# Sliding-window attention and a gated MLP on one core: two tiles of 384 tokens, one of 256 and seven of 512 instead of four of 384 and six of 512

## The chip, the core and the metric

The kernel runs on one core of one Trainium2 chip. The metric is the device time of one execution in microseconds (us). The core has five engines that run side by side and wait for one another by semaphores: TensorE (PE, matrix products into the accumulation memory PSUM), VectorE (DVE), ScalarE (ACT), GpSimd (POOL) and SyncE (SP). Transfers run on 16 DMA engines; here POOL issues all loads after the first two, and SP issues nearly all stores.

## The reference

Attention over 8 batches and 8 heads, 576 positions and 64 dimensions per head: each position sees itself and the 63 positions before it. Then a gated MLP over the 4608 tokens.

```python
scores = scale * np.matmul(q, k.transpose(0, 1, 3, 2))
rel = pos[:, None] - pos[None, :]
mask = (rel >= 0) & (rel < 64)
attn = softmax(np.where(mask, scores, -1e9))
x = np.matmul(attn, v)                       # (8, 8, 576, 64) -> (4608, 512)
gate = np.maximum(x @ w_gate, 0.0)           # 512 -> 1536
return (gate * (x @ w_val)) @ w_out          # 1536 -> 512
```

Inputs and output are fp32; the kernel computes in fp16 with fp32 accumulation.

## The kernel before

**Tiles.** The tokens are worked through in ten tiles. The first four hold 384 tokens each (two "units" of 192, or three windows of 64), the other six 512 each (two "quads" of four windows). A batch has nine windows, so tiles and batches don't line up.

**Attention.** q and k of a batch are loaded (`qk_load`, L167) and turned by DVE so that dimensions lie on the partitions (`qk_trans`, L185: four transposes per batch, k and q for each half of the heads). Both results are double-buffered by batch (`qTs`, `kTs`). v is loaded by `v_load` (L191), and `v_spread` copies it (L200, L202) so that each window finds the keys before it as well; from unit 4 on POOL makes these copies. For a window, PE computes the transposed scores (L233), ACT takes the exponential (L267 for units, L352 for quads), DVE multiplies with a band of ones (L272, L356), and PE multiplies with v (L293, L371), where a further column of ones gives the sum. DVE takes the reciprocal (L307, L386), multiplies (L317, L391) and turns the result (L327, L396) into `xt`, the input of the MLP with its dimensions on the partitions. A wide tile's result takes two pairs of PSUM banks and a further bank for what is left over ("rest").

**MLP.** `hidden` computes for each of 12 blocks of 128 hidden columns the products with w_gate and w_val (L468, four matmuls each), ACT's relu (L453) and DVE's product of both (L456). The matmuls stream all tokens of the tile. Where they are 256 or fewer, a PSUM bank holds two blocks and ACT and DVE take both at once (`w = 512 // n`). `output` multiplies each 128 tokens with w_out (L482, 12 matmuls of 512 columns), ACT copies the result out (L489), and SP stores it.

**Order.** The order of all instructions is written out by hand. `Weaver` keeps a clock in us that follows PE's work as planned: each matmul group adds its price, and `W.at(T, fn)` puts a piece of attention work in a heap with a due time. Before each group, everything due is emitted. So due times decide where in PE's stream the scores and values of the next tile stand, and in which order DVE, ACT and POOL, which run their own streams in program order, take masks, transposes, copies and gates. `pair` plans a tile of 384 and `plan_wide` a tile of 512; `loads` and `wide_loads` plan a batch's q, k and v. `ahead(t)` plans tile t + 1 and the loads of tile t + 2 when tile t begins. `ready(t)` emits what is left of tile t's attention before PE starts its hidden layer. Tile 2 is planned with due times given as constants (`pair(2, 56.0, 59.0, 62.5)`), and batch 2's loads too (`loads(3, 70.0)`: q and k at 58, v at 64, transposes at 70.0, 71.4, 72.8 and 74.2).

Of the kernel before, what the change touches and what calls it, by code (L numbers as in the profile page):

```python
# [10 lines left out]
FP32 = mybir.dt.float32  # L11
FP16 = mybir.dt.float16
# [32 lines left out]
def kernel(  # L45
# [10 lines left out]
    nc = tc.nc  # L56
    B, H, S, D = q.shape
    DM = H * D
    DF = moe_w_gate.shape[1]
    NT = B * S  # L60
    U = 192
    UB = S // U
# [4 lines left out]
    scale = 1.0 / float(D) ** 0.5  # L67
    TT = 2 * U
    WT = 512
    NS = 4  # L70
    NL = (NT - NS * TT) // WT
    assert NT == NS * TT + NL * WT and TT % 128 == 0
    starts = [TT * t for t in range(NS)] + [NS * TT + WT * t for t in range(NL)]
    widths = [TT] * NS + [WT] * NL

    consts = ctx.enter_context(tc.tile_pool(name="consts", bufs=1))
    persist = ctx.enter_context(tc.tile_pool(name="persist", bufs=1))
# [57 lines left out]
    def xt_tile(t):  # L135
        if t not in xts:
            xts[t] = x_sb.tile([128, NC, WT], FP16, name="xt")
        return xts[t]
# [75 lines left out]
    def one_bank(name):  # L214
        return f_ps.tile([128, 512], FP32, name=name, tag="h")

    def two_banks(name):
        return a_ps.tile([128, 2, 512], FP32, name=name, tag="a")
# [32 lines left out]
    def u_st(u, hhs=(0, 1)):  # L251
        d = units.setdefault(u, {})
        if "st" not in d:
            st_tiles(u)
        run_rows([[st_block(d["st"][g][:, U * hh + 64 * w:U * hh + 64 * w + 64], g, hh, UB * u + w, "biased" in d)
                   for hh in hhs for w in range(UB)] for g in range(G)])
        return 0.29 * len(hhs)
# [44 lines left out]
    def u_recip(u, hhs=(0, 1)):  # L302
        d = units[u]
        if "r" not in d:
            d["r"] = a_n.tile([128, 2, SB, 1], FP32, name="r")
        if len(hhs) == 2:
            nc.vector.reciprocal(d["r"], d["both"][:, :, 0:SB * VW].rearrange("p a (s c) -> p a s c", c=VW)[:, :, :, D:D + 1])  # L307
        else:
            hh = hhs[0]
            nc.vector.reciprocal(d["r"][:, hh], pv_of(d, u, hh)[:, :, D:D + 1])  # L310

    def u_norm(u, hh):

        d = units[u]
        if "x" not in d:
            d["x"] = a_n.tile([128, 2, SB, 2, D // 2], FP16, name="x")
        nc.vector.tensor_tensor(d["x"][:, hh], pv_of(d, u, hh)[:, :, 0:D].rearrange("p s (c e) -> p s e c", e=2),  # L317
                                d["r"][:, hh, :, :, None].to_broadcast([128, SB, 2, D // 2]), MUL)
# [11 lines left out]
            normed[0] = (u + 1) // 2 - 1  # L330

    QW = 4
    WS = 2 * WT // 64
    BS = 512 // VW
    quads = {}
    wides = {}

    def q_window(qd, i):
        return NS * TT // 64 + QW * qd + i

    def q_st(qd):

# [14 lines left out]

    def t_pv(t):

        d = wides[t] = {"pv": [two_banks("pv") for _ in range(2)], "rest": one_bank("pv"),  # L360
                        "x": a_n.tile([128, 2, WS, 2, D // 2], FP16, name="xw"), "r": a_n.tile([128, 2, WS, 1], FP32, name="rw")}
        for qh in range(2):
            qd = 2 * (t - NS) + qh
            for hh in range(2):
                for i in range(QW):
                    b, vw = divmod(q_window(qd, i), NG)
                    for s in range(2):
                        n = 2 * (QW * qh + i) + s
                        to = d["pv"][hh][:, n // BS, VW * (n % BS):] if n < 2 * BS else d["rest"][:, VW * (2 * hh + n - 2 * BS):]
                        for j in range(G):  # L370
                            nc.tensor.matmul(to[32 * j:32 * j + 32, 0:D + 1],  # L371
                                             quads[qd]["p"][j][:, QW * hh + i, 32 * s:32 * s + 32],
                                             v16s[b % 2][:, vw, G * hh + j, 0:D + 1],
                                             start=True, stop=True, skip_group_check=True)
        return 1.25

    def t_parts(d, hh):

        rest = d["rest"][:, 0:4 * VW].rearrange("p (a s c) -> p a s c", a=2, c=VW)
        return [(d["pv"][hh][:, k, 0:BS * VW].rearrange("p (s c) -> p s c", c=VW), BS * k, BS * k + BS) for k in range(2)] + [  # L380
            (rest[:, hh], 2 * BS, WS)]

    def t_recip(t, hh):
        d = wides[t]
        for pv, s0, s1 in t_parts(d, hh):
            nc.vector.reciprocal(d["r"][:, hh, s0:s1], pv[:, :, D:D + 1])  # L386

    def t_norm(t, hh, k):
        d = wides[t]
        pv, s0, s1 = t_parts(d, hh)[k]  # L390
        nc.vector.tensor_tensor(d["x"][:, hh, s0:s1], pv[:, :, 0:D].rearrange("p s (c e) -> p s e c", e=2),  # L391
                                d["r"][:, hh, s0:s1, :, None].to_broadcast([128, s1 - s0, 2, D // 2]), MUL)

    def t_turn(t, hh):
        dst = xt_tile(t)[:, 2 * hh:2 * hh + 2].rearrange("p e (s c) -> p s e c", c=32)
        nc.vector.transpose(dst, wides[t]["x"][:, hh])  # L396
        if hh == 1:
            normed[0] = t

    def plan_wide(t, TA, TB, P):  # L400
        for qd, T in ((2 * (t - NS), TA), (2 * (t - NS) + 1, TB)):
            W.at(T, lambda qd=qd: q_st(qd))
            for g in range(G):
                W.at(T + 0.8 + 0.55 * g, lambda qd=qd, g=g: q_exp(qd, g))
                W.at(T + 1.35 + 0.55 * g, lambda qd=qd, g=g: q_mask(qd, g))
        W.at(P, lambda: t_pv(t))
        for hh in range(2):
            W.at(P + 0.7 + 3.0 * hh, lambda hh=hh: t_recip(t, hh))
            for i, k in enumerate((2, 0, 1)):
                W.at(P + 1.0 + 3.0 * hh + 0.5 * i, lambda hh=hh, k=k: t_norm(t, hh, k))  # L410
            W.at(P + 2.4 + 3.0 * hh, lambda hh=hh: t_turn(t, hh))

# [5 lines left out]

    def plan_exps(T, u, mask=True, gap=0.4, first=0.8):
        for i in range(G):  # L420
            W.at(T + first + gap * i, lambda i=i: u_exp(u, i))
            if mask:
                W.at(T + first + 0.45 + gap * i, lambda i=i: u_mask(u, i))
# [106 lines left out]
    with tc.manual_schedule():  # L530
# [75 lines left out]
        W.at(43.5, lambda: v_spread(3))  # L606
        plan_values(45.0, 3)

        def pair(t, TA, TB, P):
            for u, T in ((2 * t, TA), (2 * t + 1, TB)):  # L610
                W.at(T, lambda u=u: u_st(u))
                plan_exps(T, u)
            W.at(P, lambda: u_pv(2 * t) + u_pv(2 * t + 1))
            for n in range(2):
                u = 2 * t + n
                W.at(P + 0.7 + 1.7 * n, lambda u=u: u_recip(u))
                for hh in range(2):
                    W.at(P + 0.9 + 0.5 * hh + 1.7 * n, lambda u=u, hh=hh: u_norm(u, hh))
                W.at(P + 1.9 + 1.7 * n, lambda u=u: u_turn(u))

        def loads(t, T):
            for u in (2 * t, 2 * t + 1):
                b, uu = divmod(u, UB)
                if uu == 0:
                    plan_batch(b, T - 12.0, (T, T + 1.4, T + 2.8, T + 4.2))
                W.at(T - 6.0, lambda u=u: v_load(u))
                W.at(T + 1.0, lambda u=u: v_spread(u, pool))

        for u in (4, 5):
            W.at(52.0, lambda u=u: v_spread(u, pool))  # L630
        pair(2, 56.0, 59.0, 62.5)
        def wide_loads(t, T):
            w0 = q_window(2 * (t - NS), 0)
            b = (w0 + 2 * QW - 1) // NG
            us = list(range(UB * b, UB * b + UB)) if w0 <= NG * b else []
            if t == NS:
                us.insert(0, UB * b - 1)
            if w0 <= NG * b:
                plan_batch(b, T - 12.0, (T, T + 1.4, T + 2.8, T + 4.2))
            for u in us:  # L640
                W.at(T - 6.0, lambda u=u: v_load(u))
                W.at(T + 1.0, lambda u=u: v_spread(u, pool))

        def ahead(t):
            T = W.clock
            if t + 1 < NS:
                pair(t + 1, T + 11.0, T + 14.0, T + 17.5)
            elif t + 1 == NS:
                plan_wide(t + 1, T + 9.5, T + 13.0, T + 16.2)
            elif t + 1 < NS + NL:  # L650
                plan_wide(t + 1, T + 12.0, T + 17.0, T + 22.5)
            if NS <= t + 2 < NS + NL:
                wide_loads(t + 2, T + 36.5 if t >= NS else T + 28.5)

        W.at(15.0, lambda: loads(3, 70.0))
        T = 67.0
        W.advance(15.3)
        hidden(0, ((0, U), (U, TT)), 0, 4, 4)
        hidden(0, ((0, TT),), 4, NF, 4)
# [2 lines left out]
        ready(1)  # L662
        hidden(1, ((U, TT),))
        output(1)
        for t in range(2, NS + NL):
            ready(t)
            ahead(t)
            hidden(t, ((0, widths[t]),))
            (output if t < NS + NL - 1 else output_last)(t)
        W.drain()  # L670


# [28 lines left out]
```

## Time and profile before

The median of three runs is 324.61 us (324.60 to 324.67). The profiled execution has a span of 322.9 us.

| engine | busy, us | share of the span |
|---|---|---|
| TensorE matmul | 314.3 | 97% |
| TensorE weight load | 169.1 | 52% |
| VectorE | 191.7 | 59% |
| ScalarE | 127.3 | 39% |
| GpSimd | 94.0 | 29% |

| what TensorE does | matmuls | busy, us |
|---|---|---|
| hidden layer, L468 | 1088 | 223.9 |
| output, L482 | 420 recorded | 93.9 |
| scores, L233 | 1152 | 12.9 |
| values, L293 and L371 | 1152 | 12.9 |

Busy times of matmul groups overlap[...]; what a group costs is read from the distance of its start to the next one's. [...] Idle time of DVE, ACT or POOL costs nothing unless TensorE waits at the end of it.

### The profile page before, as it was taken

How to read it: one execution, taken by the hardware profiler on the slowest of the kernel's cores; microseconds unless marked ns; L12 is line 12 of the kernel's file. 1: busy time of each engine (PE TensorE's matmuls, PEld its weight loads, DVE VectorE, ACT ScalarE, POOL GpSimd, SP SyncE). 2: the span in 40 equal slices, each digit the busy share in tenths (PEclk: the TensorE clock that was granted, in tenths of full speed). 3: DMA queues.
4: the chain of work that ended last, by engine and by line, in shares of the span. 5: the costliest groups of instructions: out<-in, count | busy, mean ns of one | idle time of the engine just before them, and what ended most of it. 6: DMA issues, size and time to landing. Idle time of an engine off the chain costs nothing.

```text
span 322.9 us, 8919 instructions
## 1 busy us (share of the span) xinstructions
PE 314.3 (97%) x3863; PEld 169.1 (52%) x3863; DVE 191.7 (59%) x369; ACT 127.3 (39%) x250; POOL 94.0 (29%) x138
## 2 busy tenths in 40 slices
PE   6699999999999999999999999999999999999996
PEld 2586958656556644454445444454445444544444
DVE  5947962587838759564765656673767145724410
ACT  3444325534424523542354234613371337223322
POOL 8766335295800290029100920081000000000000
PEclk9699999999999999999999999999999999999999
DMA  7999999989590169009910892092001200020002
GB/s 215 183 196 209 195 109 179 151 151 162 94 200 3 11 101 192 3 7 121 216 12 2 108 207 22 2 113 79 0 2 38 97 0 2 6 109 19 0 35 98
DMA packets 52488, 29.48 MB, mean 91 GB/s; under 512 B 38880, under 2 KB 43872, under 8 KB 52448
## 3 DMA queue, kind: packets, MB, share of 16 engines
q0 software_dynamic: 46688, 18.29, 48.3%
q1 hardware_dynamic: 5616, 10.55, 9.0%
q8 instruction: 30, 0.49, 0.6%
q10 hardware_dynamic: 144, 0.07, 0.1%
q14 instruction: 10, 0.08, 0.1%
HBM read 37.75 MB, written 9.44 MB: 146 GB/s over the span
## 4 chain that ended last, share of the span: by engine, by line
PE 96%; DVE 2%; DMA 1%; ACT 0%; issue 0%; DVEq 0%
PE h L468 59%; PE op L482 28%; PE st L233 3%; PE pv L371 2%; PE pv L293 2%; DMA k<-in_k_dram 1%; PE op L514 1%; DVE qT L185 1%; DVE kT L185 1%; ACT k L178 0%; DVE q L178 0%; PE st L207 0%; ACT p L267 0%; ACT o_last L517 0%; DVEq L185 0%
## 5 line engine op out<-in xcount | busy, mean ns | idle before, releaser
L456 DVE TENSOR_TENSOR g_sb<-r_sb,h 128x512 f16<-128x512 f32 (+1 forms) x120 | 75.4, 631 | 86.3 <-PE h L468 84.5
L468 PE MATMUL h<-xt,wg 128*128 128x512 f16 (+2 forms) x544 | 112.6, 339 | 0.1
L468 PE MATMUL h<-xt,wv 128*128 128x512 f16 (+2 forms) x544 | 111.3, 335 | 0.0
L453 ACT ACTIVATE r_sb<-h 128x512 f32<-128x512 f32 (+1 forms) x120 | 66.7, 558 | 89.5 <-PE h L468 81.2
L482 PE MATMUL op<-wo,g_sb 128*128 128x512 f16 x420 | 93.9, 379 | 0.0
L468 PEld LDWEIGHTS <-wg 128*128 128x128 f16 x544 | 51.7, 99 | 42.7 <-issue 0.5
L468 PEld LDWEIGHTS <-wv 128*128 128x128 f16 x544 | 50.5, 98 | 40.8
L482 PEld LDWEIGHTS <-g_sb 128*128 128x128 f16 x420 | 40.3, 98 | 47.1
L191 POOL DMA_DIRECT2D v<-in_v_dram x41 | 34.7, 862 | 94.8 <-PE pv L371 90.1
L489 ACT COPY o_sb<-op 128x512 f32<-128x512 f32 x35 | 20.5, 586 | 84.7 <-PE op L482 84.5
L356 DVE TENSOR_TENSOR pw<-pw,mask 128x512 f16<-128x512 f16 x48 | 19.3, 422 | 14.6 <-ACT pw L352 14.3
L352 ACT ACTIVATE pw<-st 128x512 f16<-128x512 f32 x48 | 25.7, 605 | 5.0 <-PE st L233 4.5
L200 POOL COPY v<-v 64x512 f16<-64x512 f16 (+1 forms) x21 | 15.4, 734 | 23.8 <-DMA v<-in_v_dram 23.0
L185 DVE STREAM_TRANSPOSE kT<-k 128x576 f32<-128x576 f32 x16 | 19.9, 1246 | 0.2 <-ACT k L178 0.2
L185 DVE STREAM_TRANSPOSE qT<-q 128x576 f32<-128x576 f32 x16 | 19.3, 1239 | 0.1
L267 ACT ACTIVATE p<-st 128x384 f16<-128x384 f32 (+1 forms) x40 | 14.0, 441 | 8.2 <-PE st L233 8.1
L391 DVE TENSOR_TENSOR xw<-pv,rw 128x448 f16<-128x448 f32 (+1 forms) x36 | 16.3, 507 | 0.4
L202 POOL COPY v<-v 64x512 f16<-64x512 f16 (+1 forms) x21 | 16.0, 760 | 1.0
L233 PEld LDWEIGHTS <-kT 32*128 32x128 f16 x1152 | 10.7, 94 | 10.2 <-issue 8.1
L233 PE MATMUL st<-qT,kT 32*128 32x64 f16 x1152 | 12.9, 192 | 3.2 <-DVE qT L185 3.2
L396 DVE STREAM_TRANSPOSE xt<-xw 128x1024 f16<-128x1024 f16 x12 | 14.9, 1245 | 0.4
L272 DVE TENSOR_TENSOR p<-p,mask 128x384 f16<-128x384 f16 x24 | 9.1, 400 | 3.5 <-ACT p L267 3.2
(45 smaller groups left out, 99.2 us busy)
## 6 DMA issues: line engine op xcount, KB each, us to landing
out_dram<-o_sb SPq DMA_DIRECT2D x35, 256.0 KB, 2.8
k<-in_k_dram POOLq DMA_DIRECT2D x15, 288.0 KB, 5.2
q<-in_q_dram POOLq DMA_DIRECT2D x15, 288.0 KB, 7.9
v<-in_v_dram POOLq DMA_DIRECT2D x31, 128.0 KB, 8.7
wg<-in_moe_w_gate_dram POOLq DMA_DIRECT2D x6, 256.0 KB, 6.4
wv<-in_moe_w_val_dram POOLq DMA_DIRECT2D x6, 256.0 KB, 8.0
wo<-in_moe_w_out_dram POOLq DMA_DIRECT2D x3, 512.0 KB, 12.3
v<-in_v_dram POOLq DMA_DIRECT2D x10, 64.0 KB, 5.9
```

The costliest lines, as they stand in the source:

```text
L185: nc.vector.transpose(dst.rearrange("p (i j) -> p j i", i=32)[:, j0:j1], src[:, j0:j1])
L191: nc.gpsimd.dma_start(v16s[b % 2][lo:hi, g, :, 0:64], v[b, :, 64 * g - 64 + lo:64 * g - 64 + hi].rearrange("h p d -> p h d"))
L202: copy(t[0:64, g0:g1:2, h0:h1, 0:64], t[64:128, g0 - 1:g1 - 1:2, h0:h1, 0:64])
L233: return [lambda dh=dh: nc.tensor.matmul(to, kTs[b % 2][rows, hh, 64 * w:64 * w + 128, dh], qTs[b % 2][rows, hh, 64 * w:64 * w + 64, dh], ...
L352: nc.scalar.activation(d["p"][g].rearrange("p n c -> p (n c)"), d["st"][g], ACT.Exp, scale=scale)
L356: nc.vector.tensor_tensor(p, p, mask[:, None, :].to_broadcast([128, 2 * QW, 64]), MUL)
L391: nc.vector.tensor_tensor(d["x"][:, hh, s0:s1], pv[:, :, 0:D].rearrange("p s (c e) -> p s e c", e=2), d["r"][:, hh, s0:s1, :, None].to_bro ...
L453: nc.scalar.activation(part(r_sb), part(h1), ACT.Relu)
L456: nc.vector.tensor_tensor(g_sb[:, f:f + w, c0:c0 + n], part(r_sb), part(h2), MUL)
L468: nc.tensor.matmul(h[:, b * n:b * n + n], wt[:, c, (f + b) * 128:(f + b) * 128 + 128], xt[:, c, c0:c0 + n], start=(c == 0), stop=(c == NC ...
L482: nc.tensor.matmul(op, g_sb[:, f, bass.ds(sub * 128, 128)], wo[:, f], start=(f == 0), stop=(f == NF - 1))
L489: nc.scalar.copy(o_sb, op)
```

## The change

Tiles 2 and 3, of 384 tokens each, become one tile of 256 tokens and one of 512, so that seven tiles are wide. The tile of 256 is planned by `plan_wide` with one quad instead of two: its results fit in the two pairs of banks, so it takes no "rest" bank, and each half of the heads has two pieces to normalise. Tiles after the second are all made of quads, so `pair` and `loads` go; units remain in the first two tiles. While the tile of 256 runs, `ahead` plans the tile of 512 after it with tighter due times (scores at 1.5 and 5.0, values at 10.6 us after its start), since it lasts half as long. Batch 2, which tile 3 needs, has due times 11 us earlier: q and k at 47, v at 53, transposes at 59.0, 60.4, 61.8 and 63.2. All masks after the first two units are multiplied in by VectorE as before. The purpose is a more uniform tiling, in which more of the kernel runs in the steady pattern of the wide tiles.

```diff
--- before.py
+++ after.py
@@ -67,11 +67,11 @@
     scale = 1.0 / float(D) ** 0.5
     TT = 2 * U
     WT = 512
-    NS = 4
-    NL = (NT - NS * TT) // WT
-    assert NT == NS * TT + NL * WT and TT % 128 == 0
-    starts = [TT * t for t in range(NS)] + [NS * TT + WT * t for t in range(NL)]
-    widths = [TT] * NS + [WT] * NL
+    NS = 2
+    widths = [TT] * NS + [WT // 2]
+    widths += [WT] * ((NT - sum(widths)) // WT)
+    starts = [sum(widths[:t]) for t in range(len(widths))]
+    assert sum(widths) == NT and TT % 128 == 0
 
     consts = ctx.enter_context(tc.tile_pool(name="consts", bufs=1))
     persist = ctx.enter_context(tc.tile_pool(name="persist", bufs=1))
@@ -330,13 +330,15 @@
             normed[0] = (u + 1) // 2 - 1
 
     QW = 4
-    WS = 2 * WT // 64
     BS = 512 // VW
     quads = {}
     wides = {}
 
     def q_window(qd, i):
         return NS * TT // 64 + QW * qd + i
+
+    def t_quads(t):
+        return [(starts[t] - starts[NS]) // 256 + i for i in range(widths[t] // 256)]
 
     def q_st(qd):
 
@@ -357,10 +359,11 @@
 
     def t_pv(t):
 
-        d = wides[t] = {"pv": [two_banks("pv") for _ in range(2)], "rest": one_bank("pv"),
-                        "x": a_n.tile([128, 2, WS, 2, D // 2], FP16, name="xw"), "r": a_n.tile([128, 2, WS, 1], FP32, name="rw")}
-        for qh in range(2):
-            qd = 2 * (t - NS) + qh
+        ws = widths[t] // 32
+        d = wides[t] = {"pv": [two_banks("pv") for _ in range(2)], "rest": one_bank("pv") if ws > 2 * BS else None,
+                        "x": a_n.tile([128, 2, WT // 32, 2, D // 2], FP16, name="xw"),
+                        "r": a_n.tile([128, 2, WT // 32, 1], FP32, name="rw")}
+        for qh, qd in enumerate(t_quads(t)):
             for hh in range(2):
                 for i in range(QW):
                     b, vw = divmod(q_window(qd, i), NG)
@@ -374,31 +377,37 @@
                                              start=True, stop=True, skip_group_check=True)
         return 1.25
 
-    def t_parts(d, hh):
-
-        rest = d["rest"][:, 0:4 * VW].rearrange("p (a s c) -> p a s c", a=2, c=VW)
-        return [(d["pv"][hh][:, k, 0:BS * VW].rearrange("p (s c) -> p s c", c=VW), BS * k, BS * k + BS) for k in range(2)] + [
-            (rest[:, hh], 2 * BS, WS)]
+    def t_parts(t, hh):
+
+        d, ws = wides[t], widths[t] // 32
+        parts = []
+        for s0 in range(0, min(ws, 2 * BS), BS):
+            n = min(BS, ws - s0)
+            parts.append((d["pv"][hh][:, s0 // BS, 0:n * VW].rearrange("p (s c) -> p s c", c=VW), s0, s0 + n))
+        if ws > 2 * BS:
+            rest = d["rest"][:, 0:4 * VW].rearrange("p (a s c) -> p a s c", a=2, c=VW)
+            parts.insert(0, (rest[:, hh], 2 * BS, ws))
+        return parts
 
     def t_recip(t, hh):
         d = wides[t]
-        for pv, s0, s1 in t_parts(d, hh):
+        for pv, s0, s1 in t_parts(t, hh):
             nc.vector.reciprocal(d["r"][:, hh, s0:s1], pv[:, :, D:D + 1])
 
     def t_norm(t, hh, k):
         d = wides[t]
-        pv, s0, s1 = t_parts(d, hh)[k]
+        pv, s0, s1 = t_parts(t, hh)[k]
         nc.vector.tensor_tensor(d["x"][:, hh, s0:s1], pv[:, :, 0:D].rearrange("p s (c e) -> p s e c", e=2),
                                 d["r"][:, hh, s0:s1, :, None].to_broadcast([128, s1 - s0, 2, D // 2]), MUL)
 
     def t_turn(t, hh):
-        dst = xt_tile(t)[:, 2 * hh:2 * hh + 2].rearrange("p e (s c) -> p s e c", c=32)
-        nc.vector.transpose(dst, wides[t]["x"][:, hh])
+        dst = xt_tile(t)[:, 2 * hh:2 * hh + 2, 0:widths[t]].rearrange("p e (s c) -> p s e c", c=32)
+        nc.vector.transpose(dst, wides[t]["x"][:, hh, 0:widths[t] // 32])
         if hh == 1:
             normed[0] = t
 
     def plan_wide(t, TA, TB, P):
-        for qd, T in ((2 * (t - NS), TA), (2 * (t - NS) + 1, TB)):
+        for qd, T in zip(t_quads(t), (TA, TB)):
             W.at(T, lambda qd=qd: q_st(qd))
             for g in range(G):
                 W.at(T + 0.8 + 0.55 * g, lambda qd=qd, g=g: q_exp(qd, g))
@@ -406,7 +415,7 @@
         W.at(P, lambda: t_pv(t))
         for hh in range(2):
             W.at(P + 0.7 + 3.0 * hh, lambda hh=hh: t_recip(t, hh))
-            for i, k in enumerate((2, 0, 1)):
+            for i, k in enumerate(range(3 if widths[t] == WT else 2)):
                 W.at(P + 1.0 + 3.0 * hh + 0.5 * i, lambda hh=hh, k=k: t_norm(t, hh, k))
             W.at(P + 2.4 + 3.0 * hh, lambda hh=hh: t_turn(t, hh))
 
@@ -606,35 +615,14 @@
         W.at(43.5, lambda: v_spread(3))
         plan_values(45.0, 3)
 
-        def pair(t, TA, TB, P):
-            for u, T in ((2 * t, TA), (2 * t + 1, TB)):
-                W.at(T, lambda u=u: u_st(u))
-                plan_exps(T, u)
-            W.at(P, lambda: u_pv(2 * t) + u_pv(2 * t + 1))
-            for n in range(2):
-                u = 2 * t + n
-                W.at(P + 0.7 + 1.7 * n, lambda u=u: u_recip(u))
-                for hh in range(2):
-                    W.at(P + 0.9 + 0.5 * hh + 1.7 * n, lambda u=u, hh=hh: u_norm(u, hh))
-                W.at(P + 1.9 + 1.7 * n, lambda u=u: u_turn(u))
-
-        def loads(t, T):
-            for u in (2 * t, 2 * t + 1):
-                b, uu = divmod(u, UB)
-                if uu == 0:
-                    plan_batch(b, T - 12.0, (T, T + 1.4, T + 2.8, T + 4.2))
-                W.at(T - 6.0, lambda u=u: v_load(u))
-                W.at(T + 1.0, lambda u=u: v_spread(u, pool))
-
         for u in (4, 5):
             W.at(52.0, lambda u=u: v_spread(u, pool))
-        pair(2, 56.0, 59.0, 62.5)
+        plan_wide(NS, 55.5, None, 59.5)
+
         def wide_loads(t, T):
-            w0 = q_window(2 * (t - NS), 0)
+            w0 = q_window(t_quads(t)[0], 0)
             b = (w0 + 2 * QW - 1) // NG
             us = list(range(UB * b, UB * b + UB)) if w0 <= NG * b else []
-            if t == NS:
-                us.insert(0, UB * b - 1)
             if w0 <= NG * b:
                 plan_batch(b, T - 12.0, (T, T + 1.4, T + 2.8, T + 4.2))
             for u in us:
@@ -642,18 +630,15 @@
                 W.at(T + 1.0, lambda u=u: v_spread(u, pool))
 
         def ahead(t):
-            T = W.clock
-            if t + 1 < NS:
-                pair(t + 1, T + 11.0, T + 14.0, T + 17.5)
-            elif t + 1 == NS:
-                plan_wide(t + 1, T + 9.5, T + 13.0, T + 16.2)
-            elif t + 1 < NS + NL:
+            T, span = W.clock, 33.6 * widths[t] / WT
+            if t == NS:
+                plan_wide(t + 1, T + 1.5, T + 5.0, T + 10.6)
+            elif t + 1 < len(widths):
                 plan_wide(t + 1, T + 12.0, T + 17.0, T + 22.5)
-            if NS <= t + 2 < NS + NL:
-                wide_loads(t + 2, T + 36.5 if t >= NS else T + 28.5)
-
-        W.at(15.0, lambda: loads(3, 70.0))
-        T = 67.0
+            if t + 2 < len(widths):
+                wide_loads(t + 2, T + span + 2.9)
+
+        W.at(15.0, lambda: wide_loads(NS + 1, 59.0))
         W.advance(15.3)
         hidden(0, ((0, U), (U, TT)), 0, 4, 4)
         hidden(0, ((0, TT),), 4, NF, 4)
@@ -662,11 +647,11 @@
         ready(1)
         hidden(1, ((U, TT),))
         output(1)
-        for t in range(2, NS + NL):
+        for t in range(NS, len(widths)):
             ready(t)
             ahead(t)
             hidden(t, ((0, widths[t]),))
-            (output if t < NS + NL - 1 else output_last)(t)
+            (output if t < len(widths) - 1 else output_last)(t)
         W.drain()
```

## The prediction

> **What bounds the kernel now.** I read the busy shares first, then what TensorE (PE) waits for, then the chain in order of time, and last VectorE (DVE) and GpSimd (POOL) in order of time around the tiles that change.
>
> ```profile
> PE 314.3 (97%) x3863; PEld 169.1 (52%) x3863; DVE 191.7 (59%) x369; ACT 127.3 (39%) x250; POOL 94.0 (29%) x138
> PE   6699999999999999999999999999999999999996
> PEclk9699999999999999999999999999999999999999
> ```
> ```profile
> PE st L233 <- DVE qT L185: 3.2, 2, 1.6
> PE st L207 <- DVE zero L544: 2.3, 1, 2.3
> ```
>
> The first fence has PE busy in every slice after the second (8.07 us each), at full clock; the second, PE's whole list of waits, has nothing but waits at the start (the score blocks at L233 that waited began at 8.97 and 11.14 us). So from about 15 us to the end PE never stands still, and an edit can only gain by giving PE less work, or lose by making it wait. The chain (start, length, what) shows the price of each piece:
>
> ```profile
> 67.89 11.05 PE h L468 x68
> 78.94 0.48 PE st L233 x40
> ...
> 84.67 0.86 PE op L482 x4
> 85.53 0.94 PE pv L293 x83
> 86.47 7.01 PE op L482 x32
> 93.48 9.75 PE h L468 x60
> 103.23 0.61 PE st L233 x58
> ...
> 109.88 1.23 PE pv L371 x118
> ...
> 119.63 12.09 PE h L468 x56
> ```
>
> Tile 2 (384 tokens) runs from 67.89 to 93.48, tile 3 to 119.63, and the next tile of 512 begins at 153.52, 33.89 us later. A score block is 0.48 us (three windows) or 0.61 (four), a value block 0.94 (two units) or 1.23 (a wide tile).
>
> [...] groups of four start 0.864 us apart at 512 columns (216 ns each), 0.650 at 384 (162.5) and 0.331 at 192 (82.8). [...] in the DVE timeline three masks take 1.72 us while POOL copies values (78.57 to 83.44 us), and 0.88 afterwards; one mask is 765 ns where the median is 359.
>
> ```profile
> 80.88 1.72 DVE L272 TENSOR_TENSOR p<-p,mask 128x384 f16<-128x384 f16 x3
> 84.09 0.88 DVE L272 TENSOR_TENSOR p<-p,mask 128x384 f16<-128x384 f16 x3
> ...
> 113.17 1.24 DVE L396 STREAM_TRANSPOSE xt<-xw 128x1024 f16<-128x1024 f16 x1
> 114.33 0.27 DVE L386 RECIPROCAL rw<-pv 128x7 f32<-128x7 f32 x3
> 114.64 1.35 DVE L391 TENSOR_TENSOR xw<-pv,rw 128x128 f16<-128x128 f32 x3
> 116.03 1.25 DVE L396 STREAM_TRANSPOSE xt<-xw 128x1024 f16<-128x1024 f16 x1
> ```
>
> **PE's work.** Two tiles of 384 become one of 256 and one of 512: 768 tokens either way, ten tiles either way. Hidden layer: before 2 x 96 matmuls x 162.5 ns = 31.20 us; after 96 x 109.3 ns + 96 x 216 ns = 31.23. Output: 72 matmuls of 512 columns either way. Scores: each block also costs about 0.09 us ahead of it (a group ahead of one lasts 0.74, not 0.65), so four blocks of three windows (4 x 0.57 = 2.28) become three of four (3 x 0.70 = 2.10). Values: 2 x (0.94 + 0.10) = 2.08 becomes 1.33 for the wide tile plus about 0.72 for half of one, 2.05. Sum: **-0.18 us**. Relu and gate fall from 120 to 114 of each (two banks' worth per instruction at 256), but ACT and DVE don't bind, so that is nothing.
>
> **Does anything make PE wait?** Four places have little slack. Positions come from the planner's clock, worked out by hand and fixed by the trace: the clock stands at about 49.65 when tile 1's second half starts (49.98 in the chain).
>
> (a) Tile 2's value block. Its one quad of scores is due at 55.5, so it falls after 18 groups: 49.98 + 18 x 0.331 + 0.09 = 56.03, ending 56.64. In the trace the last mask of a quad ends about 3.05 us after its scores (103.84 to 106.9), with relu and gate between: 59.7 here. The value block follows six groups of hidden layer and six output matmuls (1.99 + 1.30): 60.03. Slack 0.3 us, were it not for POOL. The values of batch 2 now come earlier. POOL stands idle from 35.8 to 45.1:
>
> ```profile
> 35.11 0.69 POOL L191 DMA_DIRECT2D v<-in_v_dram x1 [0.51 <-DMA q<-in_q_dram]
> 45.10 0.61 POOL L200 COPY v<-v 64x512 f16<-64x512 f16 x1 [9.31 <-DMA v<-in_v_dram]
> ...
> 48.08 1.10 POOL L167 DMA_DIRECT2D k<-in_k_dram  x2
> ...
> 62.17 1.04 POOL L200 COPY v<-v 64x1024 f16<-64x1024 f16 x1 [9.26 <-DMA v<-in_v_dram]
> ```
>
> K and q of batch 2, now due at 47, go into that hole, ahead of the copies due at 52. They are issued after all of W_out and the values of batch 1, so they queue behind these and disturb none; the transfers then run from about 45 to 54 (they took 9 us from 50 before), and the five of v land by 58. POOL's copies of them run from about 55.8 to 60.5, right over the masks (57.2 to 59.7). A mask then loses 0.1 to 0.4 us. Only the last one's loss counts, the others sit in ACT's shadow. **Cost: 0 to 0.4, I take 0.1.**
>
> (b) Tile 2's first hidden matmul, the narrowest place. The four transposes of batch 2's k and q (due 59.0 to 63.2, before at 70 and later) now share DVE with tile 2's normalisation (due 60.2 to 64.9), and DVE works in program order. From the last mask at 59.95: four transposes at 1.09 pitch, 4.36; reciprocals 2 x 0.2; normalisations 2 x 0.7 (a bank of 448 about 0.5, a block of 64 about 0.2); two turns of 512 at 0.61 (between 0.48 for 384 and 1.16 for 1024), 1.22. Sum 7.38, so xt is complete near 67.4. PE comes to tile 2 at 60.03 + 0.72 + 30 x 0.2165 = 67.2 and needs the second half of heads two matmuls later, at 67.4 or so. **Cost: 0 to 0.8, I take 0.2.** Were the four transposes not there, xt would be ready at 63.
>
> (c) Tile 3's second quad of scores, due 3.5 us after the first. It reuses the first's banks, which are free when the four exps are done, 2.5 us after the scores end (103.85 to 106.36). At 256 columns it comes 6 x 0.437 = 2.62 after. Tile 4 had the same spacing before and didn't wait. **0 to 0.2, I take 0.1.**
>
> (d) Tile 3's normalisation inside tile 2, which now lasts 18.4 us, not 25.6. The value block ends three groups and 24 output matmuls ahead of tile 3: 1.31 + 5.20 = 6.5 us. From tile 4's rows the second turn ends 6.17 after its value block (111.11 to 117.28), so xt is in time. But by the clock the first turn (due P + 2.4 = 13.0 after the tile's start) goes ahead of tile 2's last gate (13.2). That gate is then done 0.3 + 3.2 = 3.5 after the value block, and output matmul ten, the first that needs it, comes at 1.31 + 2.17 = 3.48. **0 to 0.5, I take 0.1.**
>
> From tile 3 on the plan is the steady one of 33.89 us, with batch 3's values loaded after tile 3's value block; POOL's wait there holds only the copies for tile 4, 25 us before they are used. The end is unchanged. Sum: -0.18 + 0.1 + 0.2 + 0.1 + 0.1 = **+0.3 us, so 324.9 us**, 0.1% above 324.61.
>
> **Rivals.** *No wait at all:* the slacks hold, and only PE's work counts: 324.4. For it: ready times and needs lie within 0.3 us of each other everywhere and the kernel has shown no such wait. Against it: DVE's queue of 7.4 us in a row. *Clearly slower:* POOL blocks the last mask for a whole copy (0.6), this shifts DVE's row, tile 2 waits 0.8, and tile 3's start adds 0.5: -0.18 + 1.9, 326.3. For it: the 765 ns mask; against: a late value block makes PE late too, so the waits partly overlap. *Faster:* if a matmul of 256 columns took 103 ns instead of 109 (96 x 6 ns = 0.58 us less) and nothing waited, -0.76: 323.85. Against it: 192, 384 and 512 columns all lie on one line, and PE has no idle time to give back after 15 us.
>
> **How the numbers follow.** Forecast (small waits, net between -0.1 and +0.65) 0.45; no wait 0.27; clearly slower 0.23; faster 0.05. The bound of 0.2% is 0.65 us. Forecast and no-wait lie inside it, so no change is 0.72, slower 0.23, faster 0.05. The range runs from 324.3 (no wait, a little under) to 326.0 (most of the bad ends of a, b and d together).
>
> **What would show it.** Right: tile 2's first hidden matmul at 67.2 to 67.6, tile 3's about 86, the first wide tile after it about 119.8 against 119.63, then 33.89 per tile; the DVE row of transposes and turns unbroken from 60 to 67.5; masks at 57 to 60 longer than 0.42. Waits of PE h on DVE xt, or PE pv on DVE pw, of some tenths. Wrong: a wait above 1 us at tile 2 or 3, the pitch at 256 columns off 109 ns, k or q of batch 2 landing after 59, or a later tile that isn't 33.89.

## The result and the profile after

The changed kernel takes 325.66 us (median of six runs, 325.15 to 325.98) against 324.64 us for the kernel before; the ratio is 1.0026, with a 95% interval from 1.0013 to 1.0038. It is slower by about 1 us. The profiled span went from 322.9 to 323.8 us.

The overview shows nothing: TensorE (PE) is busy for 97% of the span as before. The list of what PE waits for is longer by three lines (us in total, times, longest).

```profile
PE 313.7 (97%) x3863; PEld 168.4 (52%) x3863; DVE 189.3 (58%) x363; ACT 125.7 (39%) x240; POOL 94.0 (29%) x138
```

```profile
PE pv L374 <- DVE pw L358: 0.4, 1, 0.4
PE pv L374 <- issue: 0.4, 1, 0.4
PE h L477 <- issue: 0.2, 1, 0.2
```

The chain in order of time (start, length, what) puts them in their places. Line numbers moved: L233 still is scores, L374 values, L477 hidden layer, L491 output, L358 the masks, L465 the gate.

```profile
49.95 5.94 PE h L477 x72
55.90 0.69 PE st L233 x59
57.20 0.82 DVE pw L358
58.74 0.83 DVE pw L358
61.10 6.58 PE op L491 x30
67.68 1.75 PE h L477 x16
...
73.38 4.91 PE h L477 x44
78.29 1.11 PE pv L374 x106
80.07 1.42 PE h L477 x12
81.48 5.30 PE op L491 x24
86.78 12.09 PE h L477 x56
...
120.62 12.09 PE h L477 x56
```

Tile 1's second half starts at 49.95 us (49.98 before), and token 1536, the first of tile 4 in both tilings, at 120.62 (119.63 before). The whole loss lies between these two points: 70.67 us against 69.65. Inside it, two value blocks cost 1.2 us more than their matmuls. Tile 2's starts at 59.82, stops after three matmuls and ends near 61.1 instead of 60.5, with DVE's masks in the chain. Tile 3's, at 78.29, takes 1.78 us to 80.07 instead of 1.23. The profile gives no releaser for the second gap, only "issue". PE in order of time:

```profile
59.82 0.21 PE L374 MATMUL pv<-v,pw 128*32 128x65 f16 x3
60.42 0.68 PE L374 MATMUL pv<-v,pw 128*32 128x65 f16 x61 [0.39 <-DVE pw L358]
...
78.22 1.18 PE L374 MATMUL pv<-v,pw 128*32 128x65 f16 x114
79.77 0.30 PE L374 MATMUL pv<-v,pw 128*32 128x65 f16 x14 [0.36 <-issue]
```

### The profile page after: what moved, and what is told of

It is laid out like the page before. It is cut to its first block, busy times and chain, and to the rows that moved or that the text cites. A ratio compares the mean times of both kernels' runs of the same rounds, so it can differ in the third digit from the quotient of the medians.

```text
span 323.8 us, 8890 instructions
## 1 busy us (share of the span) xinstructions
PE 313.7 (97%) x3863; PEld 168.4 (52%) x3863; DVE 189.3 (58%) x363; ACT 125.7 (39%) x240; POOL 94.0 (29%) x138
## 4 chain that ended last, share of the span: by engine, by line
PE 94%; DMA 2%; DVE 1%; POOL 1%; issue 1%; ACT 0%; DVEq 0%; POOLq 0%
PE h L477 58%; PE op L491 28%; PE st L233 3%; PE pv L374 3%; DMA v<-in_v_dram 2%; PE pv L293 1%; PE op L523 1%; DVE pw L358 1%; DVE g_sb L465 0%; POOL v L191 0%; POOL k L167 0%; ACT pw L354 0%; DVE v L200 0%; POOL q L167 0%; PE st L207 0%
## 5 line engine op out<-in xcount | busy, mean ns | idle before, releaser
L465 DVE TENSOR_TENSOR g_sb<-r_sb,h 128x512 f16<-128x512 f32 (+1 forms) x114 | 74.6, 657 | 89.0 <-PE h L477 86.9
L477 PE MATMUL h<-xt,wg 128*128 128x512 f16 (+3 forms) x544 | 111.5, 337 | 0.3 <-issue 0.2
L477 PE MATMUL h<-xt,wv 128*128 128x512 f16 (+3 forms) x544 | 110.3, 335 | 0.0
L462 ACT ACTIVATE r_sb<-h 128x512 f32<-128x512 f32 (+1 forms) x114 | 65.7, 579 | 89.9 <-PE h L477 83.2
L491 PE MATMUL op<-wo,g_sb 128*128 128x512 f16 x420 | 93.8, 379 | 0.0
L477 PEld LDWEIGHTS <-wg 128*128 128x128 f16 x544 | 51.2, 98 | 42.8 <-issue 0.5
L477 PEld LDWEIGHTS <-wv 128*128 128x128 f16 x544 | 50.7, 98 | 41.0
L491 PEld LDWEIGHTS <-g_sb 128*128 128x128 f16 x420 | 40.2, 98 | 47.6 <-DVE g_sb L465 0.4
L498 ACT COPY o_sb<-op 128x512 f32<-128x512 f32 x35 | 20.5, 585 | 86.4 <-PE op L491 82.8
L358 DVE TENSOR_TENSOR pw<-pw,mask 128x512 f16<-128x512 f16 x60 | 24.9, 436 | 18.0 <-ACT pw L354 17.5
L354 ACT ACTIVATE pw<-st 128x512 f16<-128x512 f32 x60 | 32.0, 607 | 6.8 <-PE st L233 6.4
L400 DVE TENSOR_TENSOR xw<-pv,rw 128x448 f16<-128x448 f32 (+2 forms) x46 | 19.7, 479 | 0.0
L405 DVE STREAM_TRANSPOSE xt<-xw 128x1024 f16<-128x1024 f16 (+1 forms) x16 | 18.8, 1176 | 0.5
L202 POOL COPY v<-v 64x512 f16<-64x512 f16 (+1 forms) x21 | 16.1, 767 | 1.0
L233 PE MATMUL st<-qT,kT 32*128 32x64 f16 x1152 | 12.8, 192 | 3.7 <-DVE qT L185 3.7
L233 PEld LDWEIGHTS <-kT 32*128 32x128 f16 x1152 | 10.7, 94 | 10.2 <-issue 8.0
L374 PEld LDWEIGHTS <-pw 128*32 128x32 f16 x960 | 8.8, 94 | 4.2 <-issue 3.2
L374 PE MATMUL pv<-v,pw 128*32 128x65 f16 x960 | 9.9, 196 | 0.8 <-DVE pw L358 0.4
```

The costliest lines, as they stand in the source:

```text
L233: return [lambda dh=dh: nc.tensor.matmul(to, kTs[b % 2][rows, hh, 64 * w:64 * w + 128, dh], qTs[b % 2][rows, hh, 64 * w:64 * w + 64, dh], ...
L354: nc.scalar.activation(d["p"][g].rearrange("p n c -> p (n c)"), d["st"][g], ACT.Exp, scale=scale)
L358: nc.vector.tensor_tensor(p, p, mask[:, None, :].to_broadcast([128, 2 * QW, 64]), MUL)
L374: nc.tensor.matmul(to[32 * j:32 * j + 32, 0:D + 1], quads[qd]["p"][j][:, QW * hh + i, 32 * s:32 * s + 32], v16s[b % 2][:, vw, G * hh + j, ...
L462: nc.scalar.activation(part(r_sb), part(h1), ACT.Relu)
L465: nc.vector.tensor_tensor(g_sb[:, f:f + w, c0:c0 + n], part(r_sb), part(h2), MUL)
```

## The experiments

The theory after the first trace had two parts. First, GpSimd's (POOL's) copies of batch 2's values block the masks. Second, TensorE waits for its own instructions in tile 3's value block. The trace has a queue of kind "instruction" (q8) that brings 30 packets of 16,384 bytes; 7,726 TensorE instructions (3863 matmuls and as many weight loads) over 30 packets are about 258 for each. The rivals were a hidden data wait, DVE's row of transposes, and chance.

All experiments are measured by the same three stretches of the chain: from the start of tile 1's second half to tile 2, tile 2 itself, and the next 512 tokens (for the kernel before, with other tiles, only the sum compares).

| run | to tile 2 | tile 2 | tile 3 | sum | median, us | ratio to before (95%) |
|---|---|---|---|---|---|---|
| before | | | | 69.65 | 324.64 | |
| changed | 17.73 | 19.10 | 33.84 | 70.67 | 325.66 | 1.0026 (1.0013 to 1.0038) |
| repeated | 17.49 | 19.29 | 33.83 | 70.61 | 325.73 | 1.0024 (1.0013 to 1.0036) |
| q, k of batch 2 late | 17.15 | 20.66 | 33.84 | 71.65 | 327.55 | 1.0083 (1.0055 to 1.0111) |
| transposes early | 17.92 | 19.53 | 33.83 | 71.28 | 325.91 | 1.0035 (1.0023 to 1.0047) |
| tile 3's values early | 17.34 | 20.13 | 33.83 | 71.30 | 326.31 | 1.0040 (1.0028 to 1.0052) |
| 28 matmuls of padding | 17.16 | 18.61 | 33.84 | 69.61 | 327.06 | 1.0069 (1.0057 to 1.0081) |
| values of batch 2 first | 17.15 | 18.62 | 33.83 | 69.60 | 324.81 | 1.0002 (0.9992 to 1.0012) |
| padding, values first | 17.15 | 18.61 | 33.84 | 69.60 | 326.59 | 1.0055 (1.0042 to 1.0068) |
| before, padded | | | | 69.88 | 326.60 | 1.0063 (1.0051 to 1.0075) |
| batch 3 late | 17.76 | 18.61 | 34.83 | 71.20 | 326.44 | 1.0053 (1.0038 to 1.0068) |
| values first, tile 3's early | 17.16 | 18.54 | 33.83 | 69.53 | 324.44 | 0.9994 (0.9986 to 1.0002) |
| before, batch 2 sooner | | | | 69.66 | 324.60 | 0.9997 (0.9989 to 1.0005) |

**The changed kernel once more.** 

> The changed kernel once more, nothing edited. Two value blocks lost about 0.6 us each in its first trace: tile 2's (waiting for the last mask) and tile 3's (a gap of 0.36 us that the profile calls issue). If both are built into the order of the work, both come back and the time is again 0.8 to 1.2 us above the kernel before. If the gap in tile 3's value block is a chance event of one execution, only the first comes back in the trace (tile 4 then starts about 120.1, not 120.6).

Both waits came back: the value block of tile 2 waits less (the stretch to tile 2 is 17.49 us, not 17.73), the gap in tile 3's is 0.54 us, at the same matmul. So it is no chance event.

**Batch 2's q and k after the copies.** 

> Batch 2's q and k due at 53 instead of 47, so that POOL issues them after its copies of units 4 and 5, as in the kernel before; transposes and all else as changed. The values of batch 2 land later and POOL's copies of them start after 61 us instead of 56, past tile 2's masks. Theory (POOL's copies block the masks and so hold up tile 2's value block): masks are back at 0.42 us, the value block takes 0.6 instead of 1.2 us, and the time falls by 0.5 us against the changed kernel. Rival (the masks are late for ACT's or DVE's own order, and copies only happen to lie beside them): masks may be shorter, but the value block still waits 0.3 us or more and the time is the same within 0.2 us.

```diff
-        W.at(15.0, lambda: wide_loads(NS + 1, 59.0))
+        W.at(15.0, lambda: wide_loads(NS + 1, 59.0, 53.0))
```

The third number is the due time of q and k.

The mask part held. With the copies at 62.9 us and later, DVE's masks of tile 2 are at their usual length, and the stretch to tile 2 falls to 17.15 us. Batch 2's transfers are still in flight over the masks here (POOL's first copy waits for them until 62.9 us), so it is the copies that lengthen masks, not the transfers. POOL's copies and DVE in order of time in the changed kernel, and then DVE here:

```profile
57.13 0.61 POOL L202 COPY v<-v 64x512 f16<-64x512 f16 x1
57.80 0.69 POOL L200 COPY v<-v 64x512 f16<-64x512 f16 x1
58.53 0.76 POOL L202 COPY v<-v 64x512 f16<-64x512 f16 x1
```
```profile
57.20 0.82 DVE L358 TENSOR_TENSOR pw<-pw,mask 128x512 f16<-128x512 f16 x1 [1.30 <-ACT pw L354]
57.94 0.54 DVE L465 TENSOR_TENSOR g_sb<-r_sb,h 128x384 f16<-128x384 f32 x1
58.40 1.16 DVE L358 TENSOR_TENSOR pw<-pw,mask 128x512 f16<-128x512 f16 x2
```
```profile
57.66 0.43 DVE L358 TENSOR_TENSOR pw<-pw,mask 128x512 f16<-128x512 f16 x1 [1.30 <-ACT pw L354]
58.00 0.55 DVE L465 TENSOR_TENSOR g_sb<-r_sb,h 128x384 f16<-128x384 f32 x1
58.46 0.76 DVE L358 TENSOR_TENSOR pw<-pw,mask 128x512 f16<-128x512 f16 x2
```

The expected gain did not come: the median is 1.9 us above the changed kernel's. In the profiled execution (326.97 us, 1.45 above the changed kernel's) 0.98 us of it lie in the three stretches, because the other wait grew. Another 0.46 us lie before them: tile 1's second half starts at 50.41 us, and TensorE's granted clock rises from half to full at 18.2 us instead of 16.1. What the other executions lost beyond that is not shown. The gap in tile 3's value block is 1.46 us, and one of 0.28 us stands before it in the hidden layer:

```profile
76.65 0.28 issue
...
79.75 1.46 issue
81.20 0.30 PE pv L374 x14
```

**The transposes earlier.** 

> Batch 2's four transposes due at 51.0 to 55.2 instead of 59.0 to 63.2, while DVE has only a gate every 1.3 us; loads as changed. This takes 4.4 us out of DVE's row between tile 2's value block and tile 2. Theory (that row was hidden, PE came to tile 2 without a wait): xt is ready 4 us sooner and the time is the same within 0.2 us. Rival (the row holds PE at tile 2 or 3): the time falls by 0.3 us or more.

```diff
-                plan_batch(b, T - 12.0, (T, T + 1.4, T + 2.8, T + 4.2))
+                R = turn or T
+                plan_batch(b, T - 12.0, (R, R + 1.4, R + 2.8, R + 4.2))
```

Here `turn` is 51.0 for batch 2. DVE ends tile 2's normalisation at 64.6 us instead of 67.6, and the time stays the same (325.91 against 325.73 in the repeat). DVE's row of transposes and turns was hidden: neither trace has a wait of the hidden layer for `xt`. The last transpose now pushed the first mask to 57.70, so that the wait for the masks is still there; in this trace it and the gap (0.78 us) are a little longer than in the repeat's.

**Tile 3's value block earlier.** 

> Tile 3's value block due 9.5 instead of 10.6 us after tile 2's start, so two groups of the hidden layer earlier; its masks are ready by then. DVE's first turn for tile 3 then ends before tile 2's last gate is due, and the gate is not held up. Theory (gap inside tile 3's value block is a stall of PE's instruction stream, bound to the place in the stream or to chance): the 0.1 us in front of output matmul ten goes, and the gap stays or moves: 0.1 us less, up to 0.5 if the gap goes with the place. Rival (the value block waits for the spare bank, whose last user is a gate): with the block earlier the gap grows to 0.8 us or more, and the time is 0.3 us or more longer.

```diff
-                plan_wide(t + 1, T + 1.5, T + 5.0, T + 10.6)
+                plan_wide(t + 1, T + 1.5, T + 5.0, T + 9.5)
```

The gap grew to 1.44 us, as the rival had it, and the time by 0.6 us. But it is not the rival's wait: the gap moved from 14 matmuls before the end of the value block to 6, and 20 instead of 12 hidden matmuls follow until the output. So it stayed 26 matmuls ahead of tile 2's output; the value block moved past it. Counted in recorded TensorE instructions, the gap stands after number 2497 in this run, in the changed kernel, in its repeat, in the runs with late q and k and with early transposes. The small gap of the late run stands after 2241, and one at the start of tile 0 after 449. These differ by 256 and by 8 x 256. That is about the 258 instructions that fall to one packet, and a wait for data would have moved with the value block.

**Padding.** 

> The changed kernel with 28 more warm-up matmuls (64 columns, on zeros, no result used) among the first ones, where TensorE waits for q and k anyway. They move every later TensorE instruction 56 places down its stream; nothing else differs. Theory (the gap in tile 3's value block is TensorE waiting for its own next block of 256 instructions, 16 KB that the trace shows arriving in the queue of kind instruction; a block that holds nearly the whole value block, 256 instructions in 1.2 us, is used up before the next one is there): with 56 fewer of its instructions in that block the gap of 0.4 to 0.8 us goes, tile 2 lasts 18.5 us instead of 19.1 to 19.5. At the start another block boundary moves too, by the same theory: up to 1 us either way there, which the same padding in the kernel before measures by itself. Rival (a data wait that the profile doesn't show): the gap stays where it is in the work.

```diff
         heat(6, units[0]["st"][3])
+        heat(28, units[0]["st"][3][:, 0:64])
```

Tile 2 falls to 18.61 us without a gap, as expected. But against the expectation more changed than the place in the stream. TensorE runs about 2 us late from the start on, and POOL doesn't: it issues batch 3's k at 59.2 us instead of 61.2, while tile 2 begins at 69.06 instead of 67.68. So POOL's copies end before the masks, and the stretch to tile 2 falls to 17.16 us as well; and batch 3's transfers end about 4 us after tile 2's start instead of 8. For the gap in tile 3's value block this run alone can't tell the place of the boundary from the timing of the transfers. The value block in one piece:

```profile
74.76 4.91 PE h L477 x44
79.67 1.23 PE pv L374 x116
80.90 1.42 PE h L477 x12
```

What the run does show is the fixed number. The stop at the start again stands after instruction 449, now in tile 0's value block, where it is 1.8 us long; this is why the kernel as a whole lost.

**The kernel before, padded.** 

> The kernel before with the same 28 warm-up matmuls. A control: its dense blocks lie 25 to 35 us apart with matmuls of 384 or 512 columns around them, so no value block should gain or lose. Any difference, up to 1 us either way, is what the shift of the block boundary does at the start (tile 0), and is to be taken off the two padded runs of the changed kernel. Rival: if padding helps here by 0.5 us or more in a value block, the gap isn't special to the changed tiling.

The control takes the same stop at the same place (1.57 us, again after instruction 449), and loses more than the 1 us that I had allowed for: it is 0.63% slower. The stop isn't all of it. In the trace tile 1's second half starts 2.29 us later than in the kernel before. Tile 0's hidden layer begins 1.27 us later, and its first 32 matmuls then take 1.03 us longer, because the stretch at half clock ends at 20.6 us instead of 17.2 (in the three padded runs at 19.5 to 20.6 us, in the ten others at 15.2 to 18.5). First the kernel before, then here:

```profile
14.74 4.00 PE L468 MATMUL h<-xt,wg 128*128 128x192 f16 x32
```
```profile
16.01 5.03 PE L468 MATMUL h<-xt,wg 128*128 128x192 f16 x32
```

The later tiles gain nothing. In both padded kernels the stop stands 11 matmuls before the end of the second value block; in the changed kernel without padding the one at the start stands after 15 hidden matmuls. Counted in TensorE's records, weight loads included, these two places lie 56 apart, exactly the instructions that were put in. So the stop is bound to the number in the stream and not to the work. The stop in the control's value block:

```profile
13.34 0.40 PE L293 MATMUL pv<-v,p 128*32 128x65 f16 x29 [0.39 <-POOL v L202]
15.32 0.35 PE L293 MATMUL pv<-v,p 128*32 128x65 f16 x11 [1.57 <-issue]
```

**Values of batch 2 first.** 

> The changed kernel with batch 2's values loaded at 47 (into GpSimd's idle time), its q and k at 52.1 and GpSimd's copies of the values at 52.2, so that copies run from about 50 to 55 us, ahead of tile 2's masks, and the transfers of batch 3 also end earlier. Theory of the masks: masks at 0.42 us, tile 2's value block without a wait, 0.2 to 0.5 us less than the changed kernel. Theory of the instruction blocks: the gap in tile 3's value block stays at 0.4 to 0.8 us, not 1.5 as with q and k alone late, since transfers are over by 75 us. Together 325.3. Rival: moving the loads only shifts the wait, 325.7 or more.

```diff
-                W.at(T - 6.0, lambda u=u: v_load(u))
-                W.at(T + 1.0, lambda u=u: v_spread(u, pool))
+                W.at(v or T - 6.0, lambda u=u: v_load(u))
+                W.at(spread or T + 1.0, lambda u=u: v_spread(u, pool))
```

For batch 2, `v` is 47.0 and `spread` 52.2; q and k are due at 52.1.

Copies run from 51.1 to 55.9 us, the masks are at 0.42 us, and both waits are gone, the second against my expectation. The stream is instruction for instruction that of the changed kernel, so the block boundary did not move; what moved is when the block came. The activity by stretch of time shows it (length, us of PE, PEld, DVE, ACT and POOL, then clock, DMA share and GB/s; the share adds up overlapping packets and can pass 1), first in the run with late q and k, then in the changed kernel, then here:

```profile
70.00:75.00 5.00, 5.00 (x105) 4.33 (x104) 3.36 (x9) 4.81 (x10) 2.41 (x3) 1.00 1.04 213
75.00:79.00 4.00, 3.72 (x86) 2.95 (x84) 2.37 (x5) 1.48 (x3) 0.00 (x0) 1.00 1.84 175
```
```profile
70.00:75.00 5.00, 5.00 (x110) 4.33 (x105) 3.36 (x8) 4.71 (x10) 0.00 (x0) 1.00 1.62 197
75.00:79.00 4.00, 4.00 (x122) 3.47 (x120) 2.48 (x6) 1.60 (x4) 0.00 (x0) 1.00 0.04 5
```
```profile
70.00:75.00 5.00, 5.00 (x106) 4.32 (x105) 3.76 (x9) 4.81 (x11) 0.00 (x0) 1.00 0.03 9
75.00:79.00 4.00, 4.00 (x155) 3.50 (x153) 1.85 (x5) 0.97 (x2) 0.58 (x1) 1.00 0.00 0
```

Batch 3's transfers end after 78 us in the first, at about 75 in the second and at about 70 in the third. The last two packets of kind instruction ahead of the gap's place start at 74.4 and 78.9 us in the first (gap 1.46), 74.1 and 77.4 in the second (gap 0.36), 70.2 and 74.2 in the third (none). In the two runs with a gap PE goes on 2.3 us after the second packet's start.

This holds in all traces. Taken in order, the packets fit the boundaries one to one: the first that at 449, the second that at 705, the ninth that at 2497, in steps of 256. In none of the thirteen traces does TensorE pass a boundary less than 2.18 us after the start of its packet. At each of the sixteen stops without a releaser it goes on 2.2 to 2.6 us after it. What differs is when the packet starts: the one for 2241 follows 1.0 to 1.2 us after TensorE has passed the boundary before it (1985) in the five runs of the changed tiling without a gap, and 4.3 to 4.8 us after it in the five with one. The next packet, the one for the value block, starts 3.3 to 4.5 us after that in all ten.

Such a packet has 0.02 MB; in the changed kernel's transfers from 77.3 to 77.8 us (packets, MB, share of 16 engines) it is the only one:

```profile
q8 instruction: 1, 0.02, 11.7%
```

**Both.** 

> Both edits together: values of batch 2 first, and 28 warm-up matmuls more. If the two waits are all that the change cost, what is left is TensorE's work, 0.2 us below the kernel before: 324.4 to 324.7, apart from what the padding does at the start. If a third cost is hidden below them, 325 or more.

The stretches are those of the values first alone, 69.60 us, so no third cost lay below. The padding's loss at the start remains: 326.59 us.

**Batch 3 late.** 

> The changed kernel with batch 3's q and k issued after its values, so behind tile 3's value block, and their transposes 6.5 us later, inside tile 3; batch 2 as changed, so GpSimd's copies still lie over tile 2's masks. Between 61 and 79 us only three value transfers are left. Theory (the block of instructions that tile 3's value block needs is fetched late because batch 3's transfers keep the DMA engines busy until 75 us): the fetch before it moves from 74 to about 70 us, the one that it needs from 77.4 to about 74, the gap goes though no instruction moved, tile 2 lasts 18.6 us, and 0.5 to 0.7 us are gained; tile 2's value block still waits for its last mask. Rival (only the place of the block boundary counts, the wait of the padded run went for that reason alone): gap 0.4 to 0.8 us as before.

```diff
-                wide_loads(t + 2, T + span + 2.9)
+                if t == NS:
+                    wide_loads(t + 2, T + span + 2.9, T + 13.8, 6.5)
+                else:
+                    wide_loads(t + 2, T + span + 2.9)
```

For batch 3, q and k are due at T + 13.8 and the transposes 6.5 us later. The gap is gone with the boundary in its old place: packets at 71.0 and 75.1 us, tile 2 in 18.61. Up to tile 3 only these loads moved, so this is the run that shows the transfers as the cause of the late fetch. The wait for the masks stays (17.76). The 0.5 us don't show in the time: the late transposes end at 99.9 us and hold up tile 4's scores, so tile 3 takes 34.83 us. A gain turned into a new wait.

**Values first, tile 3's value block early.** 

> The run with batch 2's values first, with tile 3's value block two hidden groups earlier (due 9.5). With late transfers this made the gap 1.4 us, since one block then holds the whole value block. Theory (transfers decide when the fetch starts; once they end by 70 us the fetch starts well ahead): no gap or at most 0.3 us, time as with the values first, 324.8 within 0.4. Rival (the boundary's place decides): a gap of 1 us or more comes back, 325.8.

No gap, although the boundary lies in the value block as it did in the run with a gap of 1.44 us. Tile 2 takes 18.54 us; its last gate still comes behind DVE's first turn, against what the earlier block was meant to do, but the output's 24 matmuls take 5.28 us instead of the 5.35 with values first alone. 324.44 us is the fastest measured; the interval of its ratio, 0.9986 to 1.0002, reaches just past 1.

**Batch 2 sooner in the kernel before.** 

> The kernel before, old tiling, with batch 2's q, k, v and the copies of v due 11 us earlier as in the change, its transposes left at 70. GpSimd's copies of units 6 and 7 then lie at about 56 to 59 us, over the masks of unit 4. Theory (copies cost time only where a value block follows the last mask at once): masks of unit 4 take 0.5 us instead of 0.36, but the value block comes 3 us later, so no wait: same as the kernel before within 0.3 us. Rival (loading batch 2 sooner is itself what costs, by the transfers' crowding): 0.6 us or more slower.

The three masks that lie under the copies take 1.91 us here, and nothing is lost: 324.60 us, since the value block comes at 62.9 us, 1 us after the last mask.

```profile
57.58 1.91 DVE L272 TENSOR_TENSOR p<-p,mask 128x384 f16<-128x384 f16 x3 [0.41 <-ACT p L267]
```

## Why the prediction was right in its direction and short in its size

The time lies in the range, and small waits that outweigh a small saving were the forecast; the effect is 1.02 us, where 0.3 was said. By the ratio that is 0.26%, over the bound of 0.2%, but with the bound inside its interval (0.13% to 0.38%). It lies between the forecast and the rival called clearly slower (+1.7 us), whose blocked masks came, though spread over two of them. That the time fell in the range is in part luck: two of the four waits in the sum (0.3 us) didn't come, and about 0.5 us came from a cause that isn't in it. Two readings in the prediction are loose, and nothing hangs on them: the last slice of its first fence shows PE at 6, not 9, and (b) starts from a last mask at 59.95 us where (a) has 59.7. Step by step:

- **PE's work, -0.18 us: right.** Without the two large waits (values first, tile 3's early) the stretches take 69.53 us against 69.65, with 0.08 us of (d) still in them. The 256-column matmuls were put at 109.3 ns by the author's estimate, since the kernel before has none. The pitches measured there bear it out (82.8 ns at 192 columns and 162.5 at 384 give 109.4 between them at 256), and so does the changed kernel: its groups of eight start 0.875 us apart, 109.4 ns each.
- **(a) Tile 2's value block, 0.1 us: the cause was right, the size wrong.** It cost 17.73 - 17.15 = 0.58 us in the first trace and 0.34 in the second. The step that failed is "Only the last one's loss counts, the others sit in ACT's shadow". The chain has two masks of 0.82 and 0.83 us with a gate after each: DVE works in order (mask at 57.20 us, gate at 57.94, masks from 58.40), the slack between masks was filled by gates, and so two losses of 0.4 us added up. In four traces (changed, repeated, tile 3's values early, batch 3 late) the masks are 0.81, 0.57, 0.41 and 0.84 us longer in sum than four of 0.42 us, and the stretch to tile 2 is 0.58, 0.34, 0.19 and 0.61 us longer than 17.15: each time the sum less 0.22 or 0.23 us, which is the slack that the prediction put at 0.3. In the traces masks take up to 0.82 and 0.83 us under the copies and 0.42 without, gates 0.54 us under them and 0.55 without; why the one is lengthened and the other isn't was not shown. The transfers came in the order that the prediction counted on: k and q of batch 2 landed from 47.9 to 52.1 us, behind W_out (44.4) and the values of batch 1 (46.5).
- **(b) DVE's row ahead of tile 2, 0.2 us: no wait came.** The row ends near 67.56, as worked out (67.4), but the wait of (a) delayed PE as well. Taking 4.4 us out of the row brought nothing.
- **(c) Second quad of scores, 0.1 us: nothing.** The block starts at 72.70 us, without an idle entry before it.
- **(d) The gate behind the turn, 0.1 us: right.** 24 output matmuls take 5.30 us (5.35 in other runs) instead of 5.20.
- **Missed: TensorE's own instructions, about 0.5 us.** Tile 2 took 19.10 us instead of 18.61. The prediction put this at nothing, without a reason. I counted matmuls by their time, not by their number. In tile 2 a hidden matmul takes half as long as in a wide tile (109.4 ns against 216), so instructions pass twice as fast between two blocks of scores and a value block (256 instructions in 1.2 us). Tile 2 was also given batch 3's transfers. Neither the forecast nor a rival had it.

Most boundaries show no stop: of the 29 that lie in steps of 256 from 449 on, TensorE stops without a releaser at two in the changed kernel, for 0.24 us at the start and for 0.36 us in tile 3's value block. In the five runs with a gap there it is 0.36 to 1.46 us long.

That instruction fetch makes the gap is shown by its fixed number in the stream, at the start also under padding, and by the packet ahead of every stop. That transfers decide when the fetch comes is shown by three runs that left the stream as it was and moved transfers (q and k of batch 2 late, values of batch 2 first, batch 3 late). What exactly starts a fetch, and why it came 4.3 to 4.8 us after the boundary before it, not 1.0 to 1.2, while these transfers ran, stays open.

## What to carry to other kernels

Where one engine is busy all the time, look for what its neighbours' new timing collides with: here copies moved onto masks (0.83 us instead of 0.42), and a batch's transfers onto the fetch of instructions. Count instructions per microsecond as well as time: here 256 of them passed in 1.2 us next to matmuls of 109 ns, behind a batch's transfers, and TensorE stood still for 0.36 to 1.46 us with no releaser in the profile. Such a gap is told apart by counting instructions up to it, by looking for the packet that comes ahead of it, and by moving the transfers. Moving the stream a few places tells less than it seems: here it also shifted TensorE against the loads, by about 2 us.

## What the runs showed of the hardware

- TensorE stopped at boundaries of its instruction stream: after 449, 2241 and 2497 recorded instructions, 256 or a multiple of it apart, for 0.2 to 1.8 us. The profile names no releaser; it says "issue".
- The fetch of a block was one packet of 16,384 bytes, in flight for about 0.9 us at the two gaps shown; the matmuls went on about 2.3 us after its start (77.4 to 79.77 us in the changed kernel, 78.9 to 81.20 with late q and k; 2.2 to 2.6 us at all sixteen stops).
- Twenty-eight harmless matmuls in an idle place at the start cost the kernel before 2 us: they moved a boundary into a dense value block (a stop of 1.57 us), and the stretch at half clock ended 3.4 us later (20.6 instead of 17.2 us), which cost 1.0 us.
- A mask of 128x512 in fp16 took 0.42 us alone and up to 0.85 us under POOL's copies. Not every mask loses: two of tile 2's four kept 0.41 us in the changed kernel, and copies there took up to 0.76 us instead of 0.61. The gate of 128x384 took 0.54 us under the same copies and 0.55 without.
